# Gate/up weights on a second DMA queue and two gate/up steps in token halves, in a fused S5 and GeGLU kernel

## The chip, the cores and the metric

The kernel runs on one core of one Trainium2 chip. The metric is the device time of one execution in microseconds; less is better. A core has a matrix engine (TensorE, PE in the profile), a vector engine (VectorE, DVE), a scalar engine (ScalarE, ACT), a general engine (GpSimd, POOL) and a sync engine (SyncE, SP) that here only issues DMAs. Each engine takes its own instructions in the order in which the program wrote them, and engines wait for one another by semaphores.

## The reference

For 2048 tokens x of width 512, in bfloat16, the reference normalises each token (mean and variance over the width, no scale or bias), and adds three things: the input itself, a diagonal complex state-space layer, and a gated feed-forward layer.

```python
xn = _layernorm(x, axis=-1)
# A: Bu = xn @ B_bar^T; h_t = Lam_bar * h_(t-1) + Bu_t over 2048 steps
#    y = 2 * real(h @ C^T) + xn * Dskip
# B: (gelu(xn @ w_gate) * (xn @ w_up)) @ w_down, 512 -> 1376 -> 512
return x + A(xn) + B(xn)
```

## The kernel before

The tokens are worked through in four blocks of 512, each block being four tiles of 128 tokens. The hidden width 1376 is cut into eleven strips `ft` of 128 columns (the last has 96). For each block there are a gate/up stage (`GU`), the products with B (`BU`), the scan and its rotations on VectorE (`CHAIN`), and a stage that adds the down projection and the C product in PSUM (`DN`).

Block 0 starts while its inputs and weights still arrive, and is done differently. Strips 0 to 6 (columns 0 to 895) are computed with tokens in the partitions, from centred tiles that TensorE transposes itself (`cent_T`, lines 679 to 690): first the columns 0 to 511 of tiles 0 to 2, one slice of the width at a time as the weight slices come in (`GT_k`, line 702), then what is left (`GT_mm`, line 713) in the order of lines 1011 and 1012: tile 3 with columns 0 to 255 and 256 to 511, and then, for tiles 0, 1, 2 and 3, columns 512 to 767 and 768 to 895. `GT_evac` empties each bank: a GELU on ScalarE (line 722), then a product on VectorE (line 725). Only strips 7 to 10 of block 0 are done by `GU` and `GU_rest`, from normalised tiles that a DMA transposes into `XNT[0]` (`TR`, line 737). TensorE's next stages are `BU(0)`, `BU(1)`, `GU(1)` and so on.

The weights `w_gate` and `w_up` arrive in three chunks of columns, `FC` in line 385: 0 to 511 (in four slices of the width each, lines 487 to 490), 512 to 895 and 896 to 1375 (`ld_w`, lines 492 to 495). They are called the first, the second and the third chunk here. The second is needed by the `GT_mm` of columns 512 and up, the third by strips 7 to 10: `wdeps` of line 388 gives the buffers that a matmul waits for.

All of these loads are issued by SyncE. ScalarE issues only the loads of x tiles 1 and 2 and of three small parameter rows. After the third chunk SyncE issues the transpose of the parameters (`tr_par`, line 516), the four transposes of block 0, the load of x block 1 and the transposed loads of the B matrices (line 527). GpSimd's power for `exp(log_dt)` (line 558) waits for `tr_par`, and VectorE's line 559 for that power.

The order on an engine comes from a planner in the program (`Sched`, lines 78 to 345). TensorE and SyncE keep the order in which the code names their work. On VectorE, ScalarE and GpSimd the planner places each operation by assumed durations and by due times that it counts back from the end. `order_behind` (line 129) puts one operation behind another on its engine without a semaphore; `ch` (line 947) chains the start of VectorE's work that way. The tile statistics are `stats` (lines 614 to 617), and `GATE["evTA"]` is the latest ScalarE copy of a transposed tile (line 690).

Of the kernel before, what the change touches and what calls it, by code (L numbers as in the profile page):

```python
# [348 lines left out]
NT, NB, KD, KP, KF = 16, 4, 4, 4, 11  # L349
# [6 lines left out]
def d_pe(n_list):  # L356
    return sum(n / 2.4 + 2.5 for n in n_list)
def d_dve_tt2x(n): return 100.0 + 0.52 * n
def d_dve_1x(n): return 100.0 + 1.04 * n
def d_dve_scan(n): return 90.0 + 2.08 * n  # L360
def d_dve_ts4x(n): return 220.0 + 0.26 * n
D_TINY = 160.0
def d_act(n, ptr=0): return 190.0 + 0.833 * n + 90.0 * ptr
# [3 lines left out]
def build(nc, ins, out):  # L367
    with ExitStack() as es:
        E = es.enter_context
        S = Sched(nc, es)  # L370
# [9 lines left out]
        WG = A.alloc("WG", [KD, F], BF16)  # L380
        WU = A.alloc("WU", [KD, F], BF16)
# [4 lines left out]
        WGc = [Buf("WGc%d" % i, "sbx", 10 * i, 10 * i + 1) for i in range(KD + 2)]  # L386
        WUc = [Buf("WUc%d" % i, "sbx", 100 + 10 * i, 101 + 10 * i) for i in range(KD + 2)]
# [30 lines left out]
        XTk = [[Buf("XT%d_%d" % (b, i), "xt", 4 * b + i, 4 * b + i + 1) for i in range(4)] for b in range(NB)]  # L418
        XT0 = XTk[0]
        XTr = lambda b: XTk[b]  # L420
# [50 lines left out]
        GATE = {"before_gelu": [], "nh": 0}  # L471
# [17 lines left out]
            return S.dma(lambda e: e.dma_start(W.ap[:, k, f0:f1], src[128 * k:128 * (k + 1), f0:f1]),  # L489
                         256 * (f1 - f0), writes=[Wc[k]], tag="ld_w")  # L490

        def ld_w(W, Wc, src, n):
            f0, f1 = FC[n]
            return S.dma(lambda e: e.dma_start(W.ap[:, :, f0:f1], src[:, f0:f1].rearrange("(k p) f -> p k f", p=128)),
                         1024 * (f1 - f0), writes=[Wc[KD + n - 1]], tag="ld_w")

        def ld_x0(j, queue="sync", after=()):
            return S.dma(lambda e, j=j: e.dma_start(X[j].ap, x2[128 * j:128 * (j + 1), :]), 128 * 1024, writes=[X[j]], tag="ld_x0", queue=queue, after=after)
# [3 lines left out]
        for k in range(KD):  # L502
            if k == 3:
                ld_x0(k)
            ld_wk(WG, WGc, ins["B_w_gate"], k)
            ld_wk(WU, WUc, ins["B_w_up"], k)
        ld_w(WG, WGc, ins["B_w_gate"], 1)
        ld_w(WU, WUc, ins["B_w_up"], 1)

        def load_par():  # L510
            for q, nm in enumerate(("A_log_dt", "A_Lambda_re", "A_Lambda_im")):
                GATE["par"] = S.order_behind(S.dma(lambda e, q=q, nm=nm: e.dma_start(PROW.ap[4 * q:4 * q + 4, :], ins[nm].rearrange("(s p) -> s p", p=128)),
                      1024, writes=[PROWq[q]], tag="ld_" + nm, queue="scalar", after=[half]), GATE["par"])

        def tr_par():
            S.dma(lambda e: e.dma_start_transpose(PAR.ap.rearrange("p q t -> p (q t)").unsqueeze(1), PROW16.ap), 4096,
                  reads=PROWq, writes=[PAR], tag="tr_par", issue=900.0)
# [9 lines left out]
                S.dma(lambda e, b_=b_, nm=nm: e.dma_start_transpose(b_.ap, ins[nm]),  # L527
                      1.4 * 512 * 1024, writes=[b_], tag="tr_" + nm, issue=3000.0)

        def load_W():  # L530
            ld_w(WG, WGc, ins["B_w_gate"], 2)
            ld_w(WU, WUc, ins["B_w_up"], 2)

        def load_B():
            load_T([A.sub(BBT_all, "BBTc%d" % c, c) for c in range(2)], ("A_B_re", "A_B_im"))
# [13 lines left out]
        def next_bank():  # L549
            b_ = rstate["n"] % 8  # L550
            rstate["n"] += 1
            return b_
# [56 lines left out]
        def tables_act(after_gelu):  # L609
            t = ACT(lambda e: e.activation(SC16.ap, FRC.ap, ACTF.Sin, scale=SIN_SCALE), d_act(16) + 1300, [FRC], [SC16], "sin16", after=after_gelu)  # L610
            t = ACT(lambda e: e.activation(COST.ap, A1.ap, ACTF.Sin, bias=HPI.ap, scale=-SIN_SCALE), d_act(2048), [A1, HPI], [COST], "cost", after=[t])
            return ACT(lambda e: e.activation(SINT.ap, F1.ap, ACTF.Sin, scale=-SIN_SCALE), d_act(2048), [F1], [SINT], "sint", after=[t])  # L612

        def stats(b, j):
            tt = 4 * b + j
            return (V(lambda e: e.bn_stats(ST[tt].ap, X[tt].ap), d_dve_1x(512), [X[tt]], [ST[tt]], "bnst"),  # L616
                    V(lambda e: e.bn_aggr(MVt[b][j].ap, ST[tt].ap), D_TINY, [ST[tt]], [MVt[b][j]], "bnag"))
# [9 lines left out]
        def recip(qb, rq):  # L627
            return V(lambda e: e.reciprocal(rq.ap, qb.ap), 150, [qb], [rq], "rq")
# [40 lines left out]
        def SKIP(b):  # L669
            for tt in range(4 * b, 4 * b + 4):  # L670
                xs = XN[tt % 8]
                V(lambda e, tt=tt, xs=xs: e.tensor_tensor(XD[tt].ap, xs.ap, DSKB.ap, ALU.mult),
                  d_dve_tt2x(512), [xs, DSKB], [XD[tt]], "skip")
# [156 lines left out]
            S.dma(lambda e: e.dma_start_transpose(HTt[k2][ft].ap.rearrange("p (j t) -> p j t", j=4), HR.ap),  # L830
                  1.2 * 128 * 1024, reads=HRp, writes=[HTt[k2][ft]], tag="tr_h%d" % b, issue=1200.0)

        def GU(b, fts=None):
            k2 = b % 2
            fts = list(range(KF) if fts is None else fts)
            banks = {}

            def mm(ft, W, Wc, bank, c0, c1, rd):
                m = FROWS[ft]

                def f(e):
                    ins_ = None
                    for dk in range(KD):
                        ins_ = e.matmul(PS[bank][0:m, c0:c1], W.ap[:, dk, 128 * ft:128 * ft + m], XNT[b].ap[:, dk, c0:c1],  # L844
                                        start=(dk == 0), stop=(dk == KD - 1))
                    return ins_
                PE(f, d_pe([c1 - c0] * 4), wdeps(Wc, ft) + rd, [BANK[bank]], "GU%d" % b)

            for ft in fts:
                m = FROWS[ft]  # L850
                if m < 128:
                    GU_rest(b)
                    continue
                banks[ft] = (next_bank(), next_bank())
                bg, bu = banks[ft]
                kk = (KF * b + ft) % 3
                for (W, Wc, bank) in zip((WG, WU), (WGc, WUc), banks[ft]):
                    mm(ft, W, Wc, bank, 0, 512, XTr(b))
                GATE["last_gelu"] = ACT(lambda e, bg=bg, kk=kk, m=m: e.activation(  # L859
                    GG[kk].ap[0:m, :], PS[bg][0:m, :], ACTF.Gelu_apprx_tanh),  # L860
                    d_act(512), [BANK[bg]], [GG[kk]], "gelu", after=GATE["before_gelu"])
                S.order_behind(GATE["last_gelu"], GATE.pop("evBu", None))
                ACT(lambda e, bu=bu, kk=kk, m=m: e.activation(UPB[kk].ap[0:m, :], PS[bu][0:m, :], ACTF.Copy),  # L863
                    d_act(512), [BANK[bu]], [UPB[kk]], "evU")
                V(lambda e, kk=kk, m=m, ft=ft, k2=k2: e.tensor_tensor(  # L865
                    HTt[k2][ft].ap[0:m, :], GG[kk].ap[0:m, :], UPB[kk].ap[0:m, :], ALU.mult),
                  d_dve_tt2x(512), [GG[kk], UPB[kk]], [HTt[k2][ft]], "hmul")
# [79 lines left out]
        def ch(*ops):  # L947
            for op in ops:
                tail_op[0] = S.order_behind(op, tail_op[0])
        def sub(j):  # L950
            return V(lambda e: e.tensor_scalar(XN[j].ap, X[j].ap, MVt[0][j].ap[:, 0:1], None, ALU.subtract),
                     d_dve_ts4x(512), [X[j], MVt[0][j]], [XN[j]], "sub")
        load_par()
        load_W()
        tr_par()
        S.order_behind(ACT(lambda e: e.activation(H0[3].ap[:, 0:D], X[1].ap, ACTF.Copy, scale=-1.0 / D, accum_out=NM1.ap), d_act(512) + 190,
                           [X[1]], [H0[3], NM1], "mean1"), GATE["par"])
# [31 lines left out]
        ch(*stats(0, 0)); ch(*stats(0, 1))  # L989
        op, mn0, qb0, rq0 = root(0, 0, 3)  # L990
        ch(op)
        ch(*stats(0, 3)); ch(sub(3))
        ch(recip(qb0, rq0))
        op, mn3, qb3, rq3 = root(0, 3, 4)
        ch(op)
# [27 lines left out]
        LN(1, [0, 1]); LN(1, [2, 3])  # L1023
        TR(1)
        SKIP(0)
        GU(0, [7, 8, 9, 10])
        GATE["before_gelu"] = [tables_act([GATE["last_gelu"]])]
        SKIP(1)
        BU(0)
# [8 lines left out]
        late_loads()  # L1038
        scale_C()
        GU(1, [0, 1, 2, 10, 3, 4, 5, 6, 7, 8, 9])  # L1040
        BU(2)
        CHAIN(2)
        DN(0, True)
        LN_act(3); SKIP(3)
        GU(2, [0, 1, 2, 10, 3, 4, 5, 6, 7]); TR(3); GU(2, [8, 9])
        BU(3)
        CHAIN(3)
# [9 lines left out]
def bass_parallel_sum__ssm_conv_s5__geglu_ffn__prompt_kernel(  # L1057
    nc: bass.Bass,
    A_x: bass.AP,
    A_Lambda_re: bass.AP,  # L1060
    A_Lambda_im: bass.AP,
    A_B_re: bass.AP,
    A_B_im: bass.AP,
    A_C_re: bass.AP,
    A_C_im: bass.AP,
    A_log_dt: bass.AP,
    A_Dskip: bass.AP,
    B_x: bass.AP,
    B_w_gate: bass.AP,
    B_w_up: bass.AP,  # L1070
    B_w_down: bass.AP,
    out: bass.AP,
):
    ins = {
        "A_x": A_x, "A_Lambda_re": A_Lambda_re, "A_Lambda_im": A_Lambda_im,
        "A_B_re": A_B_re, "A_B_im": A_B_im, "A_C_re": A_C_re, "A_C_im": A_C_im,
        "A_log_dt": A_log_dt, "A_Dskip": A_Dskip,
        "B_w_gate": B_w_gate, "B_w_up": B_w_up, "B_w_down": B_w_down,
    }
    build(nc, ins, out)  # L1080
# [28 lines left out]
```

## Time and profile before

| | us |
|---|---|
| median of 3 runs | 177.01 |
| lowest and highest of them | 176.86, 177.09 |
| the profiled execution, its whole time | 177.68 |
| its span, first to last instruction | 176.4 |
| TensorE busy | 172.9 (98%) |
| VectorE busy | 159.7 (91%) |
| ScalarE busy | 96.0 (54%) |
| GpSimd busy | 10.7 (6%) |

The profile is one execution. Its times are counted from its first instruction. "Landing" of a DMA is the time at which its completion reaches the semaphore. The ends of matmuls are modelled: they are pipelined, so a matmul of 512 columns is shown as 379 ns long while the next one starts 216 ns after it. An "SPq" or "ACTq" row is the issue of a DMA by that engine.

### The profile page before, as it was taken

Reading aid. Unit: us, or ns where it says so; the run is one execution under the profiler, and the core shown is the slowest. Engines: PE = TensorE matmul, PEld = TensorE weight load, DVE = VectorE, ACT = ScalarE, POOL = GpSimd, SP = SyncE. Lnnn points to the kernel's source line nnn. Section 1 sums busy time; section 2 is a strip of 40 time slices with the busy share of each in tenths; the row PEclk is TensorE's granted clock in tenths of the full one; section 3 lists DMA queues with packets and bytes.
Section 4 is the critical chain, followed back from the end, with each engine's and each line's share of the span. In section 5 each row is a group of like instructions: output and inputs, shape, how many; then the busy total and the mean of one; then the engine's idle time right before and its main releaser. Section 6 shows DMA issues by size and latency. Waiting matters only on the chain.

```text
span 176.4 us, 2522 instructions
## 1 busy us (share of the span) xinstructions
PE 172.9 (98%) x889; PEld 84.8 (48%) x889; DVE 159.7 (91%) x279; ACT 96.0 (54%) x187; POOL 10.7 (6%) x24
## 2 busy tenths in 40 slices
PE   8999899999999999999999999999999999999995
PEld 2646364744644444444644444444464444444454
DVE  5987989997999989979899999989999899999941
ACT  5476577999766899292676693000667970000000
POOL 3212120202000000001200000000000000000000
DMA  5998999495998000001115000002001000000221
GB/s 176 256 334 139 248 202 157 94 162 104 193 288 226 4 0 2 0 30 59 33 32 103 16 0 0 4 0 86 33 0 30 4 0 0 0 0 0 91 93 61
DMA packets 32421, 14.37 MB, mean 81 GB/s; under 512 B 23736, under 2 KB 32408, under 8 KB 32408
## 3 DMA queue, kind: packets, MB, share of 16 engines
q1 hardware_dynamic: 32096, 13.94, 34.6%
q10 hardware_dynamic: 312, 0.27, 0.4%
q8 instruction: 7, 0.11, 0.3%
q14 instruction: 6, 0.05, 0.1%
HBM read 6.46 MB, written 2.10 MB: 49 GB/s over the span
## 4 chain that ended last, share of the span: by engine, by line
PE 95%; DMA 2%; DVE 1%; issue 0%
PE PS L885 37%; PE PS L844 32%; PE PS L750 16%; PE PS L702 3%; PE PS L818 3%; DMA arena<-arena 2%; PE PS L934 2%; PE PS L713 1%; DVE arena L725 1%; PE PS L685 1%; DVE arena L903 0%; PE PS L941 0%
## 5 line engine op out<-in xcount | busy, mean ns | idle before, releaser
L885 PE MATMUL PS<-arena 128*128 128x512 bf16 (+3 forms) x323 | 66.2, 366 | 0.0
L844 PE MATMUL PS<-arena 128*128 128x512 bf16 x264 | 58.1, 379 | 0.9 <-DMA arena<-arena 0.9
L885 PEld LDWEIGHTS PS<-arena 128*128 128x128 bf16 (+1 forms) x323 | 30.9, 98 | 35.2
L844 PEld LDWEIGHTS PS<-arena 128*128 128x128 bf16 x264 | 25.7, 98 | 31.4 <-issue 1.1
L788 DVE TENSOR_TENSOR_SCAN arena<-arena 128x512 bf16<-128x512 f32 x32 | 38.9, 1254 | 0.0
L859 ACT ACTIVATE arena<-PS 128x512 bf16<-128x512 f32 x33 | 19.8, 599 | 26.8 <-DVE arena L903 16.7
L750 PE MATMUL PS<-arena 128*128 128x512 bf16 (+1 forms) x144 | 28.2, 355 | 0.0
L863 ACT ACTIVATE arena<-PS 128x512 bf16<-128x512 f32 x33 | 19.8, 599 | 5.6 <-PE PS L844 5.6
L750 PEld LDWEIGHTS PS<-arena 128*128 128x128 bf16 x144 | 14.1, 98 | 13.3
L877 ACT ACTIVATE PS<-arena 128x512 f32<-128x512 bf16 (+2 forms) x17 | 9.6, 581 | 19.7 <-DVE arena L903 19.0
L759 ACT ACTIVATE arena<-PS 128x512 bf16<-128x512 f32 x32 | 17.5, 595 | 1.8 <-PE PS L750 1.8
L903 DVE TENSOR_TENSOR arena<-PS,arena 128x512 bf16<-128x512 f32 (+2 forms) x17 | 10.9, 653 | 6.4 <-PE PS L885 6.4
L865 DVE TENSOR_TENSOR arena<-arena 128x512 bf16<-128x512 bf16 x33 | 13.2, 417 | 2.7 <-ACT arena L863 2.5
L777 DVE TENSOR_TENSOR arena<-arena 128x4096 bf16<-128x4096 bf16 (+1 forms) x5 | 9.2, 1858 | 0.4 <-ACT arena L612 0.4
L800 DVE TENSOR_TENSOR arena<-arena 128x4096 bf16<-128x4096 bf16 x4 | 9.2, 2288 | 0.1
L775 DVE TENSOR_TENSOR arena<-arena 128x4096 bf16<-128x4096 bf16 (+1 forms) x5 | 9.2, 1857 | 0.0
L801 DVE TENSOR_TENSOR arena<-arena 128x4096 bf16<-128x4096 bf16 x4 | 9.1, 2284 | 0.0
L722 ACT ACTIVATE arena<-PS,arena 128x256 bf16<-128x256 f32 (+1 forms) x16 | 6.6, 449 | 4.1 <-PE PS L702 2.4
L616 DVE BATCH_NORM_STATS2 arena<-arena 128x6 f32<-128x512 bf16 x12 | 7.8, 680 | 0.2 <-DMA arena<-in_A_x_dram 0.2
L713 PE MATMUL PS<-arena 128*128 128x512 bf16 (+1 forms) x40 | 7.1, 336 | 0.0
L725 DVE SCALAR_TENSOR_TENSOR arena<-PS,arena 128x256 bf16<-128x256 f32 (+1 forms) x16 | 6.3, 444 | 0.5 <-PE PS L702 0.5
L702 PE MATMUL PS<-arena 128*128 128x512 bf16 (+1 forms) x30 | 6.3, 351 | 0.0
(95 smaller groups left out, 124.2 us busy)
## 6 DMA issues: line engine op xcount, KB each, us to landing
out_dram<-arena SPq DMA_DIRECT2D x15, 128.0 KB, 1.7
arena<-in_A_x_dram SPq DMA_DIRECT2D x3, 512.0 KB, 5.4
arena<-in_B_w_down_dram SPq DMA_DIRECT2D x1, 1280.0 KB, 7.1
arena<-in_B_w_gate_dram SPq DMA_DIRECT2D x4, 128.0 KB, 3.3
arena<-in_B_w_up_dram SPq DMA_DIRECT2D x4, 128.0 KB, 3.4
arena<-in_B_w_gate_dram SPq DMA_DIRECT2D x1, 480.0 KB, 6.7
arena<-in_B_w_up_dram SPq DMA_DIRECT2D x1, 480.0 KB, 7.5
arena<-arena SPq DMA_TRANSPOSE x25, 3.1
```

What stands on the lines that cost most here:

```text
L702: PE(lambda e: e.matmul(dst, XCd(j, k), WGU[:, ws[0]:ws[-1] + 1, k, f0:f1], start=first, stop=k == KD - 1, skip_group_check=True), d_pe([w ...
L750: ins_ = e.matmul(PS[bank][:, 128 * j0:128 * j1], BBT[c][dk].ap[:, 128 * s:128 * (s + 1)], XNT[b].ap[:, dk, 128 * j0:128 * j1], start=(dk ...
L759: GATE["evBu"] = ACT(lambda e, bank=bank, k3=k3, s=s, c=c: e.activation(SSc[k3][s][c].ap, PS[bank][:, :], ACTF.Copy), d_act(512), [BANK[ba ...
L775: V(lambda e, s0=s0, s1=s1: e.tensor_tensor(TA.ap[:, s0:s1], ssb.ap[:, s0:s1], cos4[:, s0:s1], ALU.mult), d_dve_tt2x(1024 * step), [ss, CO ...
L788: V(lambda e, g=g, rb=rb, init=init: e.tensor_tensor_scan(g.ap, rb, g.ap, init, ALU.mult, ALU.add), d_dve_scan(512), [g, PA[RRr]] + ([CARc ...
L844: ins_ = e.matmul(PS[bank][0:m, c0:c1], W.ap[:, dk, 128 * ft:128 * ft + m], XNT[b].ap[:, dk, c0:c1], start=(dk == 0), stop=(dk == KD - 1))
L859: GATE["last_gelu"] = ACT(lambda e, bg=bg, kk=kk, m=m: e.activation(GG[kk].ap[0:m, :], PS[bg][0:m, :], ACTF.Gelu_apprx_tanh), d_act(512), ...
L863: ACT(lambda e, bu=bu, kk=kk, m=m: e.activation(UPB[kk].ap[0:m, :], PS[bu][0:m, :], ACTF.Copy), d_act(512), [BANK[bu]], [UPB[kk]], "evU")
L865: V(lambda e, kk=kk, m=m, ft=ft, k2=k2: e.tensor_tensor(HTt[k2][ft].ap[0:m, :], GG[kk].ap[0:m, :], UPB[kk].ap[0:m, :], ALU.mult), d_dve_tt ...
L877: ACT(lambda e: e.activation(PS[bank][:, c0:c1], X[tt].ap[:, c0:c1], ACTF.Copy), d_act(c1 - c0), [X[tt]], [BANK[bank]], "seed")
L885: ins_ = e.matmul(PS[bank][:, c0:c1], l_[:, 128 * j:128 * (j + 1)], r_[:, c0:c1], start=False, stop=last and n == len(ops) - 1, skip_group ...
L903: V(lambda e: e.tensor_tensor(OUTB[ko].ap[:, c0:c1], PS[bank][:, c0:c1], XD[tt].ap[:, c0:c1], ALU.add), d_dve_1x(c1 - c0), [BANK[bank], XD ...
```

## The change

The two loads of the third chunk no longer stand on SyncE. They are issued by ScalarE, the gate's first and the up's behind it, after the latest copy of a transposed tile on that engine (that of tile 2) and with a wait for the last of the statistics of tile 3 on VectorE. And `GU` gets a list of strips that are done in token halves: for strips 7 and 8 of block 0 the gate and up products of tokens 0 to 255 are done for both strips, and then those of tokens 256 to 511 for both. A half waits only for its two transposed tiles. What follows a strip on ScalarE and VectorE stays in whole width.

```diff
-        def ld_w(W, Wc, src, n):
+        def ld_w(W, Wc, src, n, **kw):
             f0, f1 = FC[n]
             return S.dma(lambda e: e.dma_start(W.ap[:, :, f0:f1], src[:, f0:f1].rearrange("(k p) f -> p k f", p=128)),
-                         1024 * (f1 - f0), writes=[Wc[KD + n - 1]], tag="ld_w")
+                         1024 * (f1 - f0), writes=[Wc[KD + n - 1]], tag="ld_w", **kw)
...
-        def load_W():
-            ld_w(WG, WGc, ins["B_w_gate"], 2)
-            ld_w(WU, WUc, ins["B_w_up"], 2)
+        def load_W(after):
+            g = S.order_behind(ld_w(WG, WGc, ins["B_w_gate"], 2, queue="scalar", after=after), GATE["evTA"])
+            S.order_behind(ld_w(WU, WUc, ins["B_w_up"], 2, queue="scalar", after=after), g)
...
-        def GU(b, fts=None):
+        def GU(b, fts=None, halved=()):
...
+            for h in range(2 if halved else 0):
+                for ft in halved:
+                    if h == 0:
+                        banks[ft] = (next_bank(), next_bank())
+                    for (W, Wc, bank) in zip((WG, WU), (WGc, WUc), banks[ft]):
+                        mm(ft, W, Wc, bank, 256 * h, 256 * h + 256, XTk[b][2 * h:2 * h + 2])
             for ft in fts:
...
-                banks[ft] = (next_bank(), next_bank())
+                kk = (KF * b + ft) % 3
+                if ft not in halved:
+                    banks[ft] = (next_bank(), next_bank())
+                    for (W, Wc, bank) in zip((WG, WU), (WGc, WUc), banks[ft]):
+                        mm(ft, W, Wc, bank, 0, 512, XTr(b))
                 bg, bu = banks[ft]
-                kk = (KF * b + ft) % 3
-                for (W, Wc, bank) in zip((WG, WU), (WGc, WUc), banks[ft]):
-                    mm(ft, W, Wc, bank, 0, 512, XTr(b))
...
-        load_W()
         tr_par()
...
-        ch(*stats(0, 3)); ch(sub(3))
+        st3 = stats(0, 3)
+        ch(*st3); ch(sub(3))
+        load_W([st3[-1]])
...
-        GU(0, [7, 8, 9, 10])
+        GU(0, [7, 8, 9, 10], halved=(7, 8))
```

## The prediction

> **What bounds the kernel now.** I read the chain that ended last first, in order of time, and from it the pieces of the stretch that the diff touches:
>
> ```profile
> 10.93 1.74 PE PS L713 x8
> 12.67 0.37 DVE arena L725
> ...
> 14.34 4.24 DMA arena<-arena
> 18.58 0.14 issue
> 18.72 5.34 PE PS L844 x24
> 24.06 1.32 PE PS L818 x16
> 25.38 13.85 PE PS L750 x80
> 39.23 5.18 PE PS L844 x24
> 44.41 1.32 PE PS L818 x16
> 45.73 12.09 PE PS L844 x56
> ```
>
> From 18.72 us to the end the chain is matmuls back to back: whatever moves 18.72 moves the end by as much, as long as no other engine runs out. Ahead of it stands one DMA of 4.24 us, the transpose of tile 3. TensorE's waits say the same; it has one after the start:
>
> ```profile
> PE PS L844 <- DMA arena<-arena: 0.9, 1, 0.9
> ```
>
> That 0.9 counts from the modelled end of the last `GT_mm` matmul. Starts tell more. 56 matmuls of 512 columns take 12.09 us, 0.216 each. `BU(0)` and `BU(1)` are 48 of 512 columns and 32 of 256 in 13.85 us, so 256 columns cost (13.85 - 48 x 0.216) / 32 = 0.109. The timeline has the `GT_mm` stage start at 10.77; it is 24 matmuls of 512 and 16 of 256 columns, 6.93 us. So TensorE could begin `GU(0)` at 17.70 and begins at 18.72: 1.02 us is all that there is to win here.
>
> Then I asked how the DMAs of this stretch run, from the timeline:
>
> ```profile
> 5.92 0.51 SPq L494 DMA_DIRECT2D arena<-in_B_w_up_dram  x1
> ...
> 6.47 0.51 SPq L494 DMA_DIRECT2D arena<-in_B_w_gate_dram  x1
> ...
> 7.02 0.61 SPq L494 DMA_DIRECT2D arena<-in_B_w_up_dram  x1
> ...
> 7.75 2.62 SPq L516 DMA_TRANSPOSE arena<-arena  x1
> ...
> 9.73 0.47 ACT L722 ACTIVATE arena<-PS,arena 128x256 bf16<-128x256 f32 x1 [2.38 <-PE PS L702]
> ...
> 10.42 5.19 SPq L737 DMA_TRANSPOSE arena<-arena  x4
> ```
>
> SyncE has issued the third chunk by 7.63, then spends 2.62 on `tr_par`, and starts the transposes at 10.42 although tile 0 was normalised by about 9.42 (the VectorE row starts at 9.05 and does two tiles in 0.74). ScalarE has a hole of 2.38 us ahead of 9.73. The loads by themselves, each asked by its line in a narrow window, give the up half of the second chunk:
>
> ```profile
> L494 SPq DMA_DIRECT2D arena<-in_B_w_up_dram x1: 507/507/507, 5.9 to 5.9; - x1
> DMA to landing us min/median/max: 5.9/5.9/5.9
> ```
>
> It lands at 5.9 + 5.9 = 11.8. Asked in the same way, the third chunk lands at 13.2 and 14.5 and the transposes at 15.1, 15.5, 16.1 and 18.6. DMA is busy at 0.9 to 1.1 of all sixteen engines from 8 to 12 us (table by microsecond).
>
> [...] Both queues were last in use together from 2.3 to 3.5 us, and the DMA view of that stretch reads:
>
> ```profile
> q10 hardware_dynamic: 257, 0.24, 57.7%
> q1 hardware_dynamic: 223, 0.20, 50.6%
> ```
>
> (packets, MB, share; q10 is ScalarE's queue, q1 SyncE's). SyncE's part was 0.20 of 0.44 MB, 0.46, in a total of 361 GB/s. [...]
>
> **The change part by part.**
>
> *Halves.* 16 matmuls of 512 columns (3.456 us) become 32 of 256 (3.488): +0.03. The first half is 16 matmuls, 1.74 us, so tiles 2 and 3 are needed 1.74 later than tiles 0 and 1. Strip 8's banks are written 0.87 earlier; in before they were emptied by 18.26 (VectorE row at 17.52, two products), and 0.87 after 17.70 is 18.57, so they are free. The 16 more weight loads hide beside the matmuls (98 ns against 109).
>
> *SyncE.* Two issues, 0.51 + 0.61 and the gaps, leave it: `tr_par` starts at 6.5 and not 7.75. If its 2.62 stays, it ends at 9.1 and the transposes follow their tiles: tile 0 from 9.5, tile 3 from 13.4 and not 14.34. All that is queued behind on SyncE, the load of x block 1 and the B transposes, comes up to 1 us earlier; none of it ended a wait of TensorE before, so this is worth nothing. If `tr_par` costs only about the 1.26 of another transpose, tile 0 does not start earlier either, as its normalisation decides.
>
> *ScalarE.* It issues two loads after a wait for VectorE's aggregation of tile 3, which ends at 8.29 + 0.18 = 8.47. Issues of 0.51 and 0.61 end at about 9.7. Behind them stand the first GELU (9.73) and the copy of tile 3 that starts `GT_mm`. The hole of 2.38 covers this, with 0 to 0.1 left; without that cover it would cost 1.1 on the path. I take 0.
>
> *Third chunk.* 983 KB come at 9.8 and later, the first load of the program having taken from 0.73 to 2.0 until DMA was busy (table by microsecond). They need 2.7 us at 361 GB/s, but share. The same total work was done by 16.4 to 17 in before. I expect them, and the transposes of tiles 0 and 1, by 16.5. Cover: 17.70.
>
> *Second chunk.* This is the part that I think decides. `GT_mm` does tile 3's columns 0 to 511 in 8 matmuls, 1.73 us from 10.77, and at 12.50 it needs the second chunk, which landed at 11.8: a slack of 0.7. In before the third chunk stood behind it in one queue and could not disturb it. Now it comes in by a second queue while the second chunk is still in transfer. The packet records show its last packet leave at 11.4, 0.4 ahead of landing; from 9.85 that is 1.55 us of work on the slowest DMA engine. At a share of 0.46 this becomes 3.4 us: to 13.25, landing at 13.6. Bounds: 11.8 without disturbance; 14.5 if all 2.7 us of the third chunk go first. I take 13.6. TensorE then starts 0.14 later as at 18.58, idles from 12.50 to 13.75, and the remaining 16 x 0.216 + 16 x 0.109 = 5.20 us end at 18.95, where `GU(0)` starts without a wait.
>
> *The sum*, at the start of `GU(0)`: transposes -1.02, second chunk +1.25, halves +0.03, ScalarE 0: +0.26, to a span of 176.7. The profiled execution took 177.68, 1.3 more than its span and 0.67 over the median; I put the difference on the median: 177.27.
>
> *Planner.* It knows nothing of shared queues, and thinks `tr_par` early. It may place VectorE's parameter work (line 559) ahead of products; `tr_par` would really land near 14, and GpSimd's 1.02 follows. Bounds 0 to 1.0, since banks are free for some time; I take 0.
>
> **Rivals.**
>
> *The second chunk is in time.* If the slowest DMA engine is ahead of where it was in the profile, or ScalarE's issue comes later than I think, it lands by 12.4 and the whole 1.02 is won: 176.0. Up to a landing at 13.0 the gain is over 0.35. For it: the mean DMA engine was done with this chunk 1 us ahead of the slowest. Against: the slowest counts. Worked out: 176.0 to 176.65.
>
> *The third chunk is favoured* (slower). Place: the same wait at 12.50. If ScalarE's queue is served first, as its 257 of 480 packets hint, the landing goes to 14.5, TensorE waits 2.15, and the sum is -1.02 + 2.15 + 0.03 = +1.16: 178.2. From a landing at 13.7 it is slower by over 0.35.
>
> *VectorE's order* (slower): parameter work early, VectorE held until about 15.1 with products behind it. In before it waited 1.19 for this power and nothing followed. Worked out at +0.5 to +1.0 on the forecast's path: 177.6 to 178.0.
>
> *It does not do what it says*: the second half could wait for tiles 2 and 3 in place of the first. They would have to land after 17.70 + 1.74 = 19.44, and they landed at 16.1 and 18.6 with SyncE a microsecond later than it will be. I give it nothing.
>
> **How the numbers follow.** The trade of one wait for another has a chance of 0.45, and its own range is landing at 13.2 to 14.0, 176.85 to 177.7. In time: 0.27. Favoured: 0.18. VectorE's order: 0.10. The range that leaves out 2 in 10 is 176.15 to 178.05. 0.2% is 0.35 us, about what a measurement here can tell. The trade gives 0.01 faster, 0.31 same and 0.13 slower, so in all faster 0.28, same 0.31, slower 0.41.
>
> **What would show it.** Right: TensorE's waits name line 713, waiting for a DMA from `w_up`, for 1 us or so near 12.5; the wait of line 844 for the transposes is gone; the second chunk lands past 13, the third by 16.5; SyncE's transposes begin near 9.5; ScalarE's first GELU stays at about 9.7. Wrong: a `GT_mm` stage without a hole (then 176.0), a new wait at line 844 for the third chunk, or a hole later than 20 us, which I have excluded.

## The result, and the profile after

The changed kernel takes 177.60 us, the median of 6 runs (177.37 to 178.04); beside it the kernel before took 176.90 (6 runs, 176.58 to 177.09). The ratio is 1.0046, 95% interval 1.0029 to 1.0063: slower by half a per cent. The forecast was 177.27 with a range of 176.15 to 178.05, so the range holds the time and the likeliest direction is right. The reason is not the forecast's: the loss comes from something that the forecast has no step for, so that it fell in the range is luck. The rest of this document is about the reason.

| | before | after |
|---|---|---|
| profiled execution, whole time | 177.68 | 177.98 |
| its span | 176.38 | 176.14 |
| whole time minus span | 1.30 | 1.84 |
| start of the `GT_mm` stage | 10.77 | 11.35 |
| start of `GU(0)` | 18.72 | 18.28 |
| end of the last matmul | 174.54 | 174.14 |
| from there to the end of the span | 1.84 | 2.00 |

The span of the profiled execution became shorter, not longer. Its whole time became longer, because 0.54 us more lies outside the span.

TensorE's waits of the changed kernel, after its start, are none. The view of waits has one line (the engine or line that waited, what it waited for, microseconds in all, times, longest); it is the first instruction's. Before, the wait of line 844 for a DMA stood here too.

```profile
PE PS L941 <- PEq L1102: 0.8, 1, 0.8
```

The chain that ended last says the same of the stretch in which one wait was to go and another to come. Its columns are start and duration in microseconds:

```profile
10.44 1.08 PE PS L702 x5
11.52 6.93 PE PS L713 x40
18.44 3.49 PE PS L844 x32
21.94 0.05 issue
21.99 1.67 PE PS L844 x7
23.66 1.32 PE PS L818 x16
```

All 40 matmuls of `GT_mm` run in 6.93 us, exactly the length that the prediction computed for a stage without a hole (24 x 0.216 + 16 x 0.109), and `GU(0)` follows them at once. So the trade at the heart of the forecast, one wait given for another, did not happen: neither wait is there.

The timeline of the issues shows that SyncE, ScalarE and the transposes moved much as worked out:

```profile
5.93 0.51 SPq L494 DMA_DIRECT2D arena<-in_B_w_up_dram  x1
...
6.57 1.18 SPq L516 DMA_TRANSPOSE arena<-arena  x1
...
8.87 0.40 ACTq L494 DMA_DIRECT2D arena<-in_B_w_gate_dram  x1
...
9.30 0.53 ACTq L494 DMA_DIRECT2D arena<-in_B_w_up_dram  x1
...
9.86 6.09 SPq L737 DMA_TRANSPOSE arena<-arena  x4
```

`tr_par` cost SyncE 1.18 and not 2.62, and the transposes began at 9.86 instead of 10.42. The two loads on ScalarE took 0.93 and fell into its hole: what follows them there is the copy of tile 3 at 10.47, and TensorE had done that tile's transposes only at 10.05 to 10.44. The planner now has this copy ahead of the first GELU (10.97), which in before came first, at 9.73. `GT_mm` starts at 11.35 here and at 10.98 to 11.57 in six later profiles of kernels with the third chunk on ScalarE; five profiles with the start of before have 10.75 to 11.46. The ranges overlap, but the means are 11.22 and 10.96, so a small cost of the new start isn't excluded by this. The run below with both program ends put back bounds what the whole change costs inside at about 0.2 us (upper end of its interval: 1.0011).

The loads by line, first SyncE's second chunk (gate at 5.5, up at 5.9), then ScalarE's third chunk (8.9 and 9.3):

```profile
DMA to landing us min/median/max: 5.1/5.4/5.7
```

```profile
DMA to landing us min/median/max: 5.5/5.9/6.4
```

The up half of the second chunk landed at 5.93 + 5.7 = 11.65 (11.8 before, 13.6 forecast). The third chunk landed at 14.3 and 15.7, ahead of the 16.5 forecast.

### The profile page after: what moved, and what is told of

It is laid out like the page before. It is cut to its first block, busy times and chain, and to the rows that moved or that the text cites. A ratio compares the mean times of both kernels' runs of the same rounds, so it can differ in the third digit from the quotient of the medians.

```text
span 176.1 us, 2531 instructions
## 1 busy us (share of the span) xinstructions
PE 172.5 (98%) x890; PEld 86.9 (49%) x905; DVE 159.7 (91%) x279; ACT 95.4 (54%) x187; POOL 11.1 (6%) x24
## 3 DMA queue, kind: packets, MB, share of 16 engines
q10 hardware_dynamic: 1368, 1.25, 2.4%
## 4 chain that ended last, share of the span: by engine, by line
PE 98%; issue 1%; DVE 0%
PE PS L892 37%; PE PS L844 32%; PE PS L750 16%; PE PS L713 4%; PE PS L702 3%; PE PS L818 3%; PE PS L941 2%; PE PS L685 1%; DVE arena L910 0%; PE PS L948 0%
## 5 line engine op out<-in xcount | busy, mean ns | idle before, releaser
L844 PE MATMUL PS<-arena 128*128 128x512 bf16 (+1 forms) x274 | 57.7, 367 | 0.3
L844 PEld LDWEIGHTS PS<-arena 128*128 128x128 bf16 x280 | 27.4, 98 | 28.7
L750 PE MATMUL PS<-arena 128*128 128x512 bf16 (+1 forms) x141 | 27.8, 355 | 0.2
L750 PEld LDWEIGHTS PS<-arena 128*128 128x128 bf16 x144 | 14.1, 98 | 13.3
L713 PE MATMUL PS<-arena 128*128 128x512 bf16 (+1 forms) x40 | 7.1, 336 | 0.0
L702 PE MATMUL PS<-arena 128*128 128x512 bf16 (+1 forms) x30 | 6.7, 366 | 0.0
```

The source lines that it names most:

```text
L702: PE(lambda e: e.matmul(dst, XCd(j, k), WGU[:, ws[0]:ws[-1] + 1, k, f0:f1], start=first, stop=k == KD - 1, skip_group_check=True), d_pe([w ...
L713: ins_ = e.matmul(dst, XCd(j, k), WGU[:, :, k, f0:f1], start=(k == 0), stop=(k == KD - 1))
L750: ins_ = e.matmul(PS[bank][:, 128 * j0:128 * j1], BBT[c][dk].ap[:, 128 * s:128 * (s + 1)], XNT[b].ap[:, dk, 128 * j0:128 * j1], start=(dk ...
```

## What was asked of the experiments

Two questions followed. Why did nothing come of removing the wait of 1.02 us, when the hole that was to replace it did not appear? And where do the 0.7 us come from?

On the first, the theory was that the wait of the one profile before was no property of that kernel. On the second, a look at the ends of the two traces gave a theory with two parts. The trace has one-packet transfers of 8 KB on a queue of kind "instruction" (q14); I take them for engines' refills of their own programs. The DMA view of the kernel before, from 176.4 us on, has nothing:

```profile
DMA packets 0, 0.00 MB, mean 0 GB/s; under 512 B 0, under 2 KB 0, under 8 KB 0
```

The same view of the changed kernel has one such refill, at 177.22, 1.08 us after the last instruction of the span (176.14):

```profile
DMA packets 1, 0.01 MB, mean 4 GB/s; under 512 B 0, under 2 KB 0, under 8 KB 0
...
q14 instruction: 1, 0.01, 1.6%
```

In before it came at 176.32, beside the last wait of the program. SyncE's program is the one that the change shortened: 79 instructions in the trace, against 81, since two loads left it. The second part is VectorE's: 319 instructions against 322, because the planner's new order needs fewer separate waits (39 in the trace, 42 before), and the refill that stood at 171.60 in before comes at 174.33, while SyncE issues the last stores. The timeline of SyncE at the end, first before, then after:

```profile
174.26 0.97 SPq L905 DMA_DIRECT2D out_dram<-arena  x2
```

```profile
173.86 1.13 SPq L912 DMA_DIRECT2D out_dram<-arena  x2
```

The two issues take 0.16 more, and the span ends 2.00 instead of 1.84 after the last matmul. In short, the theory: the first end is 0.5 us behind the span, from SyncE's length; the second is 0.1 to 0.2 inside it, from VectorE's. Rivals: that the second queue, the halves, or a changed order of VectorE costs time inside the span; and that the loss belongs to a chip. The trace doesn't name the engine that a refill belongs to, so the length of each program had to be changed by itself.

In the tables below, "whole time minus span" is the median over the runs of a label, the span the median of all runs, and the tail (last matmul to the end of the span) is of the profile. The kernel before, run beside each group, has 1.29 to 1.31, a span of 175.7 to 175.8 and a tail of 1.84.

## The parts of the change, one at a time

**The queue alone.** The changed kernel without the halves.

```diff
-        GU(0, [7, 8, 9, 10], halved=(7, 8))
+        GU(0, [7, 8, 9, 10])
```

> The third chunk goes over ScalarE's queue, GU(0) stays in whole width. SyncE's program is as short as in the changed kernel (79 recorded instructions, two fewer than before). Theory 1 (the loss lies outside the span: SyncE's program is two instructions shorter, so its last refill of instructions, in before at 176.32 beside the last wait, comes only after the last instruction, at 177.22 in the changed kernel): whole time minus span is 1.87 us as in the changed kernel, not 1.28. Theory 2 (the loss comes from the halves, or from TensorE's 16 more instructions): whole time minus span is 1.28 and the ratio to before is 1.000 or less. Theory 3 of the prediction (the second chunk is disturbed by the second queue): the w_up load of the second chunk lands past 13 and line 713 waits for it.

Measured: 177.77, ratio 1.0048 (1.0030 to 1.0065); whole time minus span 1.87, span 175.9, tail 2.06. SyncE has 79 instructions, VectorE 320. The up half of the second chunk landed at 11.46. The queue alone has the whole loss of the change. Of the 0.74 us between the medians (177.77 and 177.03), 0.58 lies outside the span and the rest inside. Theory 3 is out: the second chunk landed early, and the wait view names no wait of line 713.

**The halves alone.** The kernel before with the halves; the third chunk stays on SyncE.

```diff
-        GU(0, [7, 8, 9, 10])
+        GU(0, [7, 8, 9, 10], halved=(7, 8))
```

> GU(0) in halves, the third chunk stays on SyncE, whose program has its old length of 81. Theory 1: whole time minus span is 1.28 us, and the time is that of before less what the halves win, so a ratio of 0.995 to 1.000. Theory 2: whole time minus span is 1.87 and the ratio is 1.003 or more. In both the halves alone should win most of the 1.02 us of the wait for the transposed tile 3, if that wait is as long in most executions as in the profile of before.

Measured: 177.77, ratio 1.0048 (1.0032 to 1.0065). The same number by another way: whole time minus span is 1.29, as before, and the span is 176.5. Its view of waits has, after the start:

```profile
PE PS L713 <- DVE arena L725: 0.3, 1, 0.3
```

and its chain leads to this through the parameters:

```profile
7.83 7.30 DMA arena<-arena
...
15.27 1.03 POOL arena L558
...
16.39 0.06 DVE arena L559
...
16.50 0.49 DVE arena L725
```

The first line is `tr_par`, which lands at 15.13 because the third chunk is ahead of it in SyncE's queue. GpSimd's power follows, and VectorE, on which the planner now placed line 559 ahead of products, stands for it. The 0.3 of the view counts from a modelled end; by the starts the stage takes 7.40 us (11.02 to 18.42), 0.47 more than its 6.93. VectorE's timeline shows the wait (in brackets: idle time before it, and what ended it):

```profile
16.39 0.16 DVE L559 TENSOR_TENSOR arena<-arena 128x4 f32<-128x4 bf16 x1 [1.96 <-POOL arena L558]
```

This is the rival "VectorE's order" of the prediction, in its cause and in its size (+0.5 to +1.0 worked out there), but in a kernel that the prediction wasn't about. The expectation that the halves alone would win most of 1.02 us missed. In the changed kernel `tr_par` lands at 11.81, with the third chunk off SyncE, and the planner's early place costs no wait of TensorE. (VectorE there waits 1.35 for `tr_par` at line 575, while TensorE has other banks.)

**The halves, with the parameters first.** To see whether that is the cause and not the halves themselves:

```diff
-        load_W()
         tr_par()
+        load_W()
```

> The two steps in halves alone, the third chunk on SyncE, but the parameter transfer issued ahead of the three chunks. Theory (the 0.75 in the span of the halves alone comes from VectorE standing in the parameter work behind a late transfer): no wait of TensorE for VectorE at line 713, median span 175.7 to 176.0, whole time minus span 1.29, ratio 0.999 to 1.002. If the halves themselves cost, or the chunks on SyncE do: span 176.4, ratio 1.004 to 1.005.

(The edit puts `tr_par` ahead of the third chunk alone, not of three: it is issued at 6.57, after the second chunk at 5.46 and 5.94.)

Measured: 177.04, ratio 1.0002 (0.9988 to 1.0016), whole time minus span 1.29, median span 175.75. So 0.75 us in the span went with the late `tr_par`, and the halves themselves cost nothing that can be seen. The expectation missed one thing: a wait of TensorE for VectorE is still in the profile, earlier, and for another line. From its chain:

```profile
6.57 5.69 DMA arena<-arena
...
12.28 0.04 DVE arena L575
...
12.43 0.48 DVE arena L725
...
13.05 5.36 PE PS L713 x32
18.41 3.49 PE PS L844 x32
```

Here VectorE stood for `tr_par` itself, which landed at 12.26, and TensorE idled 0.36 (0.51 by the starts: 18.24 - 10.80 - 6.93). Its span in that execution is 176.0; the median of its 14 runs is the kernel before's.

## What became of the wait of 1.02

**The kernel before, once more**, with a profile.

> The kernel before itself, for the spans of its timed executions. Theory 1: whole time minus span is 1.28 us in all of them, so the spans have a median of about 175.6, and the 176.4 of the profile was a slow execution; the wait of line 844 for the transposed tile 3 is then shorter than 1.02 us in most executions.

Measured: ratio 1.0018 (0.9993 to 1.0044) to the other runs of the same kernel, whole time minus span 1.32, span 175.9. Its waits after the start and its timeline at `GU(0)`:

```profile
PE PS L934 <- PEq L1094: 0.8, 1, 0.8
```

```profile
17.89 5.34 PE L844 MATMUL PS<-arena 128*128 128x512 bf16 x24
```

For comparison, the first execution had at this place:

```profile
18.72 5.34 PE L844 MATMUL PS<-arena 128*128 128x512 bf16 x24 [0.86 <-DMA arena<-arena]
```

The same program, without the wait: tile 3's transpose landed at 16.74 and not at 18.58. The later profiles of kernels with this start (below, SyncE shorter and longer) don't have the wait either: `GU(0)` starts at 17.80 (79 instructions), 17.67 (105), and, with a late `GT_mm` at 11.46, at 18.61 (75). There the trace has only 23 of the first 24 matmuls; with the missing one the start would be 18.39, which is 11.46 + 6.93. In these three, tile 3 landed at 16.28, 16.57 and 16.82. Among 142 timed runs of the kernel before, spans have a median of 175.8, and 14 are 176.3 or more: the profiled execution, 176.4, lay in the slow end of the scatter.

What was different in it is in its DMA view from 16.4 to 16.6 us (packets, MB, share of sixteen engines):

```profile
q8 instruction: 1, 0.02, 29.2%
q1 hardware_dynamic: 8, 0.00, 4.8%
```

One packet of 16 KB of instructions, 0.93 us long, started while tile 3's transpose was in flight. In the other profiles the first such packet of this stretch comes between 18.99 and 21.28, when the transposes are done. The packet records fit: the instruction packet ends at 17.47, the last two 4-byte packets of this stretch on SyncE's queue start at 17.46 and 17.47, and of the transpose's sixteen completions fifteen came by 16.98 and one only at 18.58. That the packet held this one up is likely from the times, but no kernel was made that moves it alone, so it isn't shown. Shown is that the wait is not there in the four other profiles of kernels with this start; with the spans this says that in most executions there was nothing to win.

**The second chunk** was not disturbed, and the DMA view from 10 to 11 us says how the two queues shared. After:

```profile
DMA packets 253, 0.18 MB, mean 184 GB/s; under 512 B 34, under 2 KB 253, under 8 KB 253
...
q10 hardware_dynamic: 72, 0.07, 52.2%
q1 hardware_dynamic: 181, 0.12, 35.4%
```

The kernel before, in its second profile:

```profile
DMA packets 366, 0.30 MB, mean 304 GB/s; under 512 B 11, under 2 KB 366, under 8 KB 366
...
q1 hardware_dynamic: 366, 0.30, 101.7%
```

With one queue, q1 moves the second chunk's end and the third chunk's beginning, 0.30 MB. With two, the total fell to 0.18 MB, and q10 got 72 of 253 packets. The new queue took time on the engines (its share is the larger) without moving much. Part of the fall is only that SyncE's queue has no third chunk to move any more; the two can't be told apart here. What matters is the landing of the second chunk: 11.10 to 11.67 in the seven profiles with the third chunk on ScalarE, 11.36 to 12.12 in the seven with it on SyncE.

The packet records say in part why. The second chunk is 1024 packets of 768 bytes. In the changed kernel the first packet of the third chunk (960 bytes) starts at 9.94; at 10.0 the second chunk has 159 packets left, and 12 at 11.0. In the kernel before's first profile the third chunk's packets start even earlier, at 9.38, beside the second chunk's on the same queue, and 197 and 12 are left at those times. So the second chunk was nearly done when the third came, and up to 11.0 fewer packets of the third ran beside it (76) than in before (238). The trace doesn't name a packet's DMA engine, so whether any of the 76 came between the second chunk's on the same engine, and why the last 12 were not slowed, stays open.

## The two ends of the program

**One instruction more on SyncE.** The changed kernel with two waits on semaphores that are long since satisfied, put ahead of SyncE's first store; they become one instruction, so SyncE has 80.

```diff
+                if e == "sync" and op.tag == "st_out" and plan[e][n - 1][1].tag != "st_out" and not self.padded:
+                    self.padded = True
+                    for k in range(2):
+                        h.wait_ge(order[e][k].sem, 16)
```

> The changed kernel with two more waits on SyncE, for loads that landed long ago, ahead of the first store (SyncE is idle there for tens of us). SyncE's program has 81 instructions again. Theory 1: whole time minus span falls from 1.87 to 1.28 us, the span stays at about 175.75, so 177.0 in place of 177.6. Theory 2, and any theory that puts the cost on the use of ScalarE's queue: 1.87 stays and the time stays at 177.6.

Measured: 177.56, ratio 1.0032 (1.0017 to 1.0046), whole time minus span 1.36, down from 1.86; the refill moved to 176.81, 0.62 after the end of the span. But the expected 177.0 did not come: the span is 176.2 and not 175.75, so what was won outside was lost inside, and the time is that of the changed kernel. The tail in the profile is 2.28. VectorE's end is not all of it: SyncE's last wait is recorded at 176.17, 0.22 after the last store landed (175.95), where the other profiles have 0.01 to 0.02. With 80 instructions SyncE's end seems to cost in part inside the span; this is one profile.

**Both ends back, and each by itself.** The same idle waits, four on SyncE (81 instructions) and six on VectorE (322), ahead of the last operations:

```diff
+        pads = {"sync": ([op.tag for op in order["sync"]].index("st_out"), 4), "vector": (len(order["vector"]) - 12, 6)}
...
+                if e in pads and n == pads[e][0]:
+                    for k in range(pads[e][1]):
+                        h.wait_ge(order["sync"][k % 10].sem, 16)
```

> The changed kernel with idle waits on loads that landed long ago, so many that SyncE's program is 81 instructions long and VectorE's 322, both as in before. Theory 1, both parts (an instruction refill of SyncE after the last instruction costs 0.59 us outside the span; a refill of VectorE at 174.1 to 174.7 us lies beside the last store and lengthens the tail, from the end of the last matmul to the end of the span, from 1.84 to 2.0 us and more): whole time minus span 1.28, tail 1.84, and the time is that of before, ratio 0.998 to 1.001. If the changed order of work inside costs time too, the ratio stays at 1.002 or more.

VectorE alone (the 4 is a 0):

> The changed kernel with VectorE's program 3 instructions longer, 322 as in before, and SyncE's left at 79. The tail alone: it falls from 2.0 to 1.84 us and the span by 0.15 to 0.4, whole time minus span stays at 1.87. If VectorE's refill is not what lengthens the tail, nothing changes.

SyncE alone (the 6 is a 0):

> The changed kernel with two idle waits added to SyncE (81 instructions), VectorE left at 319. Theory: whole time minus span returns to 1.29, the last matmul to the end of the span stays at 2.0, so only the second of the two ends is left: ratio 1.000 to 1.002. If SyncE's length isn't the cause, whole time minus span stays at 1.8 and the ratio at 1.0035 to 1.005.

And the changed kernel as it is, beside the last:

> The changed kernel once more, on the chip of the next three runs (79 instructions of SyncE, 319 of VectorE). Theory (two program ends): whole time minus span 1.81 to 1.88, last matmul to end of span 2.0, median span 175.7 to 176.1, ratio 1.003 to 1.005. A rival, that the loss belongs to one chip, expects a ratio of 1.000 to 1.002 here.

Measured, with SyncE's and VectorE's instructions counted in the traces (rows one and three ran on one chip, two and four on another, each beside the kernel before):

| kernel | SyncE | VectorE | whole minus span | tail | median span | ratio to before |
|---|---|---|---|---|---|---|
| changed, again | 79 | 319 | 1.83 | 1.87 | 175.8 | 1.0043 (1.0021 to 1.0065) |
| VectorE padded | 79 | 322 | 1.81 | 1.84 | 175.9 | 1.0034 (1.0022 to 1.0047) |
| SyncE padded | 81 | 319 | 1.30 | 2.11 | 175.9 | 1.0010 (0.9999 to 1.0022) |
| both padded | 81 | 322 | 1.29 | 1.84 | 175.8 | 1.0000 (0.9988 to 1.0011) |

With both programs at their old lengths the changed kernel is as fast as the one before, to about 0.1%, with all of the change's loads, halves and new order in it. SyncE's two instructions are worth 1.83 - 1.30 = 0.53 us. The whole loss is 0.76 by the ratio of 1.0043 (its interval is 0.37 to 1.15) and 0.54 by the medians (177.63 and 177.09). They show in every run: 1.78 to 1.90 with 79 in the table's kernels, 1.25 to 1.35 with 81, no overlap. The rival that the loss belongs to one chip is out: it is there on three chips (the queue alone ran on a third). What is left over, if anything, may be VectorE's. Its sign in the profiles is clear where the refill meets the last store. SyncE's last two issues, with VectorE unpadded and SyncE padded (the refill at 173.9), and then with VectorE padded and SyncE not (at 171.4):

```profile
173.49 1.24 SPq L916 DMA_DIRECT2D out_dram<-arena  x2
```

```profile
173.78 0.97 SPq L916 DMA_DIRECT2D out_dram<-arena  x2
```

In the six profiles in which this refill starts between 173.96 and 174.67 the two issues take 1.00 to 1.24, in the eight others 0.97 or 0.98. But what it costs in time isn't settled: the changed kernel's second profile has a tail of 1.87 where 2.0 was expected, with VectorE padded alone the span did not fall as expected (175.9), and the intervals of "SyncE padded" and "both padded" overlap. With 318 instructions (the halves with the parameters first) VectorE's refill comes at 175.58, after the last store's issue, and the tail is 1.89.

**The kernel before with its end moved.** If the length of SyncE's program is the cause, the kernel before must lose by it too, without any of the change. Four of the waits for early stores, which SyncE makes near its end, go to GpSimd (79 instructions):

```diff
-                    for (s, v) in final_waits[:-4]:
+                    for (s, v) in final_waits[4:-4]:
...
+        for (s, v) in final_waits[:4]:
+            nc.gpsimd.wait_ge(s, v)
```

> The kernel before with SyncE's program two instructions shorter: four of its waits for finished stores stand on GpSimd, which is idle at the end. No load, no matmul and no queue differs. Theory 1: whole time minus span goes from 1.28 to 1.87 us, so 177.6 in place of 177.0, with the span as before (about 175.7). If the 0.59 belongs to the use of ScalarE's queue or to the halves: 1.28 stays.

Measured: 177.79, ratio 1.0035 (1.0020 to 1.0051), span 175.9, whole time minus span 1.81. The loss is there without the change. The refill comes at 176.55, again 1.08 after the end of the span (175.47). GpSimd has two instructions more here (33 against 31), so this run alone can't tell SyncE's length from GpSimd's new waits; the padded kernels above, which leave GpSimd as it is, can.

48 idle waits on SyncE, 105 instructions:

> The kernel before with SyncE's program 24 instructions longer, by idle waits ahead of the first store, so that its refill comes long before the end. If the refill at 176.3 us is still in part waited for in before, whole time minus span falls below 1.28, perhaps to 0.7, and the kernel is faster by that: 176.4. If it is fully hidden there, 1.28 stays and so does the time.

Measured: 177.04, ratio 0.9992 (0.9977 to 1.0008), whole time minus span 1.29. SyncE's refill is now at 94.14, far from the end, and nothing is won by that: in the kernel before it cost nothing already. That this packet moves with SyncE's length, while the one at 170.55 stays (170.75 in the kernel before's second profile), is the nearest that the traces come to naming its engine.

Twelve of the waits on GpSimd (as above with 12 for 4; 75 instructions):

> The kernel before with twelve of the waits for the last stores moved from SyncE to GpSimd: 75 instructions of SyncE. If any shorter SyncE program pays: whole time minus span 1.8, ratio 1.0035. If what counts is where the last refill of SyncE's instructions falls, a program this short may have none at the end, and whole time minus span is 1.3 or less, ratio 0.999 to 1.001. Span 175.5 to 175.9 in both.

Measured: 177.47, ratio 1.0013 (0.9992 to 1.0034), and neither expectation: of 14 runs, eight have a whole time minus span of 1.30 to 1.37 and six 1.64 to 1.89. In the profile (1.69) the refill is at 177.62, 1.57 after the end of the span. So it isn't "the later the refill, the longer". What is known, for the time outside the span: 81 and 105 cost nothing, 80 costs 0.06 (but the span was 0.5 longer), 79 costs 0.5 in every run of four kernels, 75 costs 0.3 to 0.6 in some runs. The refill starts at 94.14 with 105 instructions, within about 0.2 of the end of the span with 81 (five profiles), 0.62 behind that end with 80, about 1.1 behind it with 79 (four profiles) and 1.57 with 75. A cost for a refill that comes well behind the end would fit 105, 81 and 79; why 75 pays in only some runs isn't shown. That the end of an execution waits for this refill is an inference: after the span the trace has nothing but the packet.

## Why the prediction was right, and why it was wrong

The time fell in the range and the sign was the likelier one, by luck: neither wait of the forecast's sum was at work, and the cost that was had no term. By its own steps:

- **What bounds the kernel**, the wait of 1.02 as "all that there is to win": the step that failed first. It was read from one execution and was true of that one; the second profile of the same program has none. Taking -1.02 from the median 177.01 was wrong even before the change: the profile's whole time was 0.67 above the median, and this difference, which the prediction noted, is about the size of the wait. The prediction should have asked whether the wait was what made this execution slow.
- **Second chunk**, "the part that I think decides": wrong. +1.25 was forecast from a share of 0.46 against a second queue; measured is a landing at 11.65 and no hole. The share was taken from a stretch that begins with q10's first packet (2.34; q1's is at 2.00), in which q10 had 257 of 480 packets. In this one it had 72 of 253 in the first microsecond that matters, and the second chunk's last packets went through. At 10.0, just behind the third chunk's first packet, 159 of the second's 1024 were left; and in before too the third ran beside the second's end, from 9.38, where the prediction has it stand behind. That the split would be the same here was the author's estimate, and it didn't show: nothing in the transfer's landing showed a loss. That the last completion of a transfer is what counts did show in the first profile: tile 3's transpose had fifteen of its sixteen completions by 16.98 and the last at 18.58, and TensorE, which waited for it, began at 18.72. Of the second chunk's up half the mean of the sixteen is 10.71, the last 11.80.
- **The two errors cancelled**: -1.02 + 1.25 = +0.23, where the runs show neither the gain nor the cost. That is why the sum looked good.
- **The sum**, "I put the difference on the median": it treats whole time minus span as a constant, 1.3. It was the term that changed, by 0.54 in the profile and 0.52 in the runs of the last group (1.31 to 1.83). The prediction had no step for it. SyncE's two instructions were counted as relief of 1.12 us for its queue; that they shorten its program, and that the program's end could cost, appeared nowhere.
- **Halves**: +0.03 is within what can't be seen; with the parameters first the halves measure 1.0002.
- **SyncE**: the transposes were to begin at 9.5 or, with a `tr_par` of 1.26, as tile 0 allows; 1.18 and 9.86 were measured. Tile 3 landed at 17.73, later than the 16.74 of the kernel before's second profile, but before `GU(0)` began at all (18.28), so nothing depended on it.
- **ScalarE** at 0: right; 0.93 us of issues in a hole of 2.54. The first GELU didn't stay at 9.7 (it went behind the copy, 10.97), without a wait of TensorE.
- **Third chunk** by 16.5: right, 15.7.
- **Planner** at 0: right for the changed kernel, where the third chunk no longer stood ahead of `tr_par`. What the halves alone show (0.75 in the span) is within its bound of 1.0. There may also be a cost of the planner that no step had: fewer waits on VectorE, and with them a refill beside the last store (tails of 1.87 to 2.11 with SyncE at 79 or 81, against 1.84); what it costs in time isn't settled.

The prediction's own test, "wrong: a `GT_mm` stage without a hole (then 176.0)", gave the right verdict on the mechanism and the wrong time, because the 176.0 rested on the wait that most executions don't have.

## What to carry to other kernels

Before a wait of one profile is put down as a gain, compare that execution's whole time with the median of the runs: when it is slower by about the size of the wait, the wait may be that execution's alone, and a second profile of the same program decides it. Keep span and whole time apart: a change that only moves instructions between engines can leave the span as it is and lengthen what follows it (with four waits moved from SyncE to GpSimd the span was 175.9 and what lies outside it 1.81 in place of 1.30), and then padding the program's end back to its old length both shows the cause and takes the loss away (1.30 in place of 1.83 in the changed kernel). And if two parts of a change have the same total, look where each has it: here 0.48% was mostly outside the span for one and wholly inside it for the other.

## What was not expected of the hardware

- The length of SyncE's program near its end: two instructions fewer cost 0.5 us after the last instruction, in the changed kernel and in the one before; with one fewer it was 0.06, but the span was 0.5 longer; six fewer cost 0.3 to 0.6 in 6 of 14 runs.
- A refill of 8 KB beside a store: the last two issues of SyncE took 1.00 to 1.24 us in place of 0.97.
- A load on a second queue, started beside a busy one, went with 184 GB/s moved by the sixteen engines from 10 to 11 us in place of 304 (169 with the queue alone), and the older load landed no later.
